# Six heads of a decay-attention kernel go from whole to split scores; where a split head's copies and subtractions run is changed

## The chip, the cores and the metric

One core of a Trainium2 chip runs the whole program. The metric is the device time of one execution in microseconds. Five engines are spoken of: PE (TensorE, matrix products), DVE (VectorE), ACT (ScalarE), POOL (GpSimd) and SP (SyncE, which issues the DMAs). Each engine works through its own instructions strictly in the order in which they stand; engines wait for each other through semaphores.

## The reference

For 8 batches of 8 heads, with 576 positions and 64 dimensions per head:

```
scores = q @ k.T / sqrt(64)
cum    = cumsum(log(clip(f, 1e-4, 1)))
attn   = softmax over s of: scores[t, s] + cum[t] - cum[s], with s <= t
x      = attn @ v                       (heads put side by side: 4608 tokens x 512)
out    = relu(x @ w_in)**2 @ w_out      (w_in 512 x 2048, w_out 2048 x 512)
```

All of it is float32, and the kernel keeps float32 accuracy.

## The kernel before, in words

**Whole and split.** PE multiplies float32 in two ways here. A *whole* product takes float32 operands as they are; the profile shows it as two MATMUL instructions for one product, and it is slow for each column. A *split* product writes an operand x as xh + xl, where xh is x rounded to the type float32r (a CAST) and xl = x - xh (a subtraction, itself written as float32r), and multiplies the parts, each in one fast pass. The weights, the MLP's activations and heads 16 to 63 are split; heads 0 to 15 are whole (`NWHOLE = 16`).

**Scores of a head.** `score` (line 383) makes the transposed scores of a head in six units, by blocks of keys, of 320, 320, 192, 64, 448 and 256 columns. A whole head takes one float32 product a unit (L392, keys and queries in tile `rl`). A split head takes two products a unit: kl0 by r2 (L399: rounded keys and rounded queries, tile `rk`, with rows for the cumulative decay and the row maximum), and l2 by r1 (L402: tile `rl`, 128 rows, where l2 holds the keys' low part above and the rounded keys below, and r1 the rounded queries above and the queries' low part below). So for a split head, `prep` (line 305) needs four copies, r2, kl0, the lower half of l2 and the upper half of r1, and two subtractions, the upper half of l2 and the lower half of r1. Before, DVE makes r2 and kl0 (L313, L314), ACT makes the two further copies (L315, L318), and POOL makes both subtractions (L321, L324).

**Maxima.** The row maximum of each head is taken ahead of its scores, while the head before it is scored. `max_units` (line 337) multiplies a block of r2 (as the stationary operand) by kl0 on PE (L346), and DVE reduces the result (L354); it does six such units for a head. For a split head the maxima go by DMA into a row of r2 (L359). For a whole head `turn_maxima` (line 371) turns them into a row with five small products on PE (L377) and two ACT copies (L381).

**Weights of the attention.** ACT takes the exponential (L409). Split heads mask the diagonal block on POOL afterwards (L411), cast p to its high part on ACT (L424), subtract on DVE (L425) and multiply by a split v (L435 to L437). Whole heads add the mask on PE ahead of the exponential (L395) and multiply whole p by whole v (L456). At the end of a half head ACT copies the result and the denominators out of PSUM (L470, L471). `split_v` (line 326) splits v with a cast on DVE (L332) and a subtraction on POOL (L333).

**MLP.** Tokens go in 18 chunks of 256, each with 16 steps of two halves: `mlp1` (twelve matmuls at L555, then ACT L563, DVE L564, ACT L565, DVE L566) and `mlp2` (six matmuls of 512 columns at L578).

**Conversion.** The weights come in a 64-bit form. `weight_ops` (line 186) turns each of 32 blocks into float32 words on DVE (L228, L233, L236, L240) with a magnitude on ACT (L205); then ACT casts the high part (L210) and POOL subtracts for the low part (L216). An MLP step is written only after its two blocks' low parts are.

**What sets the order.** The main loop (from line 742) goes by slots, one score unit each, six to a head. In slot n it writes: the score of this unit, the product with v of two slots earlier, divisions, events of the slot's first half, conversion, MLP halves as a pace demands (`fill`), events of the second half, conversion, MLP halves. Events are fixed by tables (lines 632 to 636): `SPLIT = 0, 1, 1, 3` puts the four parts of `prep` of head h into the second halves of slots 0, 1, 1 and 3 of head h - 1; `MAXIMA` puts the six maximum units of a split head at slots 1.5 to 4, and those of a whole head at 0 to 2.5. Within one half slot `prep` is written ahead of the maximum unit. `in_order` keeps PE, ACT, DVE and POOL in the order of writing. So the order on each engine is fixed, and a wait on one instruction holds all that follows on that engine.

Of the kernel before, what the change touches and what calls it, by code (L numbers as in the profile page):

```python
# [9 lines left out]
F32 = mybir.dt.float32  # L10
# [4 lines left out]
ALU = mybir.AluOpType  # L15
# [19 lines left out]
def decay_attention_relu2_kernel(  # L35
# [35 lines left out]

    MAG_LOW, MAG_HIGH = struct.unpack("<2f", struct.pack("<2I", 0x38000000, 0x47EFFFFF))

    NWHOLE = 16
    DEPTH = 4
    cpool = ctx.enter_context(tc.tile_pool(name="cpool", bufs=1))
    wk = ctx.enter_context(tc.tile_pool(name="wk", bufs=2))
# [54 lines left out]
    def f32(x):  # L132
        return x if x.dtype == F32 else x.bitcast(F32)
# [52 lines left out]
    def weight_ops():  # L186

        staged, done = {}, {}

        def stage():  # L190
            i = len(staged)
            if i < NW:
                raw = staged[i] = wk.tile([P, 2 * DM], I32, name=f"w{i}", bufs=1)
                nc.sync.dma_start(out=raw, in_=(w_in, w_out)[i % 2][i // 2].bitcast(I32))

        def words(i):
            w = staged[i].rearrange("p (n t) -> p n t", t=2)
            return w[:, :, 0], w[:, :, 1]

        mags = {}  # L200

        def magnitude(i):
            if i < NW:
                mags[i] = wk.tile([P, DM], F32, name="wmag", bufs=1)
                nc.scalar.activation(out=mags[i], in_=words(i)[1].bitcast(F32), func=AF.Abs)  # L205

        def high_part(i):
            if i >= 0:
                hl = wk.tile([P, 2, DM], F32R, name=f"w{i}", bufs=1)
                nc.scalar.copy(out=hl[:, 0], in_=done[i])  # L210
                done[i] = done[i], hl

        def low_part(i):
            if i >= 0:
                w, hl = done.pop(i)
                nc.gpsimd.tensor_tensor(out=hl[:, 1], in0=w, in1=hl[:, 0].bitcast(F32), op=ALU.subtract)  # L216
                split_w.append(hl)

        stage()
        yield  # L220
        magnitude(0)
        stage()
        yield
        for i in range(NW):
            low, high = words(i)
            mag = mags.pop(i)

            nc.vector.tensor_scalar(mag, mag, MAG_LOW, MAG_HIGH, ALU.max, ALU.min)  # L228
            yield
            w = done[i] = wk.tile([P, DM], F32, name="osb")  # L230
            wi = w.bitcast(I32)

            nc.vector.tensor_scalar(wi, mag.bitcast(I32), 3, 0x3FFFFFFF, ALU.logical_shift_left, ALU.bitwise_and)  # L233
            high_part(i - 1)
            yield
            nc.vector.scalar_tensor_tensor(wi, high, -0x40000000, wi, ALU.bitwise_and, ALU.bitwise_or)  # L236
            low_part(i - 1)
            magnitude(i + 1)
            yield
            nc.vector.scalar_tensor_tensor(wi, low, 29, wi, ALU.logical_shift_right, ALU.bitwise_or)  # L240
# [57 lines left out]
    def load_v(h):  # L298
        if h < NH:
            vr = state[h]["vr"] = wk.tile([P, NJ, D + 2], F32, name="v", bufs=3)  # L300
            nc.sync.dma_start(out=vr[:, :, :D], in_=v[h])
            if h < NWHOLE:
                nc.gpsimd.memset(vr[:, :, D:], 1.0)

    def prep(h, part):

        if part == 0:
            x = planes(wk, F32R, "rl")
            (r2, kl0), (r1, l2) = ((x.q, x.k) for x in (rounded[h % 2], x))
# [3 lines left out]
            nc.vector.tensor_copy(out=r2[:D], in_=st["raw"][:, 0, :])  # L313
            nc.vector.tensor_copy(out=kl0[:D, :S], in_=st["raw"][:, 1, :])  # L314
            nc.scalar.copy(out=st["l2"][D:, :S], in_=st["raw"][:, 1, :])  # L315
        st = state[h]
        if part == 1:
            nc.scalar.copy(out=st["r1"][:D], in_=st["raw"][:, 0, :])  # L318
        if part == 2:
            k, l2 = st["raw"][:, 1, :], st["l2"][:D, :S]  # L320
            nc.gpsimd.tensor_tensor(out=l2, in0=k, in1=st["kl0"][:D, :S].bitcast(F32), op=ALU.subtract)  # L321
        if part == 3:
            q, r1 = st["raw"][:, 0, :], st["r1"]
            nc.gpsimd.tensor_tensor(out=r1[D:], in0=q, in1=r1[:D].bitcast(F32), op=ALU.subtract)  # L324

    def split_v(h):
        if NWHOLE <= h < NH:
            st = state[h]
            vr = st["vr"][:, :, :D]
            vh = st["vh"] = vhs[h % 2]  # L330
            st["vl"] = wk.tile([P, NJ, D], F32R, name="v", bufs=3)
            nc.vector.tensor_copy(out=vh[:, :, :D], in_=vr)  # L332
            nc.gpsimd.tensor_tensor(  # L333
                out=st["vl"], in0=vr, in1=vh[:, :, :D].bitcast(F32), op=ALU.subtract,
            )
# [47 lines left out]
    def score(h, u):  # L383
        st = state[h]
        j, q0, q1 = UNITS[u]
        k0, kn = KT[j]
        n = q1 - q0
        ps = bank("s")
        if h < NWHOLE:
            masked = q0 == k0  # L390
            r, k = st["whole"].q[:D + 3], st["whole"].k[:D + 3]
            nc.tensor.matmul(ps[:kn, :n], k[:, k0:k0 + kn], r[:, q0:q1], start=True, stop=not masked)  # L392
            if masked:
                m = min(kn, n)
                nc.tensor.matmul(  # L395
                    ps[:kn, :m], mz[:kn, MW - P:MW - P + kn], eye[:kn, :m], start=False, stop=True,
                )
        else:
            nc.tensor.matmul(  # L399
                ps[:kn, :n], st["kl0"][:D + 3, k0:k0 + kn], st["r2"][:D + 3, q0:q1], start=True, stop=False,  # L400
            )
            nc.tensor.matmul(  # L402
                ps[:kn, :n], st["l2"][:, k0:k0 + kn], st["r1"][:, q0:q1], start=False, stop=True,
            )
        if h < NWHOLE:
            p = wk.tile([P, 448], F32, name=("ph", "pl")[u % 2], bufs=3)
        else:
            p = wk.tile([P, 448], F32, name="p")
        nc.scalar.activation(out=p[:kn, :n], in_=ps[:kn, :n], func=AF.Exp, scale=SCALE)  # L409
        if h >= NWHOLE and q0 == k0:  # L410
            nc.gpsimd.affine_select(  # L411
                out=p[:kn, :min(kn, n)], in_=p[:kn, :min(kn, n)], pattern=[[1, min(kn, n)]],
                compare_op=ALU.is_ge, fill=0.0, base=0, channel_multiplier=-1,
            )
        st["p"][u] = p
# [23 lines left out]
    def av_part(h, u, low):  # L439

        j, q0, q1 = UNITS[u]
        s0, s1 = (q0, min(q1, QA)) if low else (max(q0, QA), q1)
        if s0 >= s1:
            return
        st = state[h]
        first = u == (NU - 1 if low else 0)
        last = u == NU - 2
        if first:
            st["av"] = bank("av")
        acc = st["av"]  # L450
        kn = KT[j][1]
        base = 0 if low else QA
        o, i = slice(s0 - base, s1 - base), slice(s0 - q0, s1 - q0)
        if h < NWHOLE:
            vr = st["vr"][:kn, j, :D + 1]
            nc.tensor.matmul(acc[:D + 1, o], vr, st["p"][u][:kn, i], start=first, stop=last)  # L456
        else:
            av_split(st, acc, u, o, i, first, last)
        if last:
            n = QA if low else S - QA  # L460
            if not low:
                if h % H == 0:
                    xts[h // H] = wk.tile([P, NCC, S], F32, name=f"xt{h // H % 2}", bufs=1)
                if h % 2 == 0:
                    st["den"] = wk.tile([P, S], F32, name="den")
                else:
                    st["den"] = state[h - 1]["den"]
            o = (h % 2) * D
            x = xts[h // H][o:o + D, (h % H) // 2, base:base + n]
            nc.scalar.copy(out=x, in_=acc[:D, :n])  # L470
            nc.scalar.copy(out=st["den"][o:o + 1, base:base + n], in_=acc[D:D + 1, :n])  # L471
# [270 lines left out]
    for n in range(-2 * NU, last_slot + 1):  # L742
        live = 0 <= n < len(slots)
        split_last()
        if live:
            h, u = slots[n]
            score(h, u)
            if h >= NWHOLE:
                unsplit.append((h, u))
        for ha, ua in avs.get(n, ()):  # L750
            if ua < NU - 1:
# [59 lines left out]
```

## Time and profile before

| | us |
|---|---|
| runs: median (lowest to highest) of 3 | 1220.62 (1219.54 to 1220.74) |
| the profiled execution | 1217.56 |
| its span, first to last instruction | 1215.8 |
| PE busy | 1189.4 (98%) |
| weight loads on PE (beside the matmuls) | 1047.3 (86%) |
| DVE busy | 769.5 (63%) |
| ACT busy | 706.2 (58%) |
| POOL busy | 361.8 (30%) |

Busy time of PE counts matmuls whose ends are modelled and which overlap in the pipeline, so how fast PE advances is better read from the start of one matmul to the start of the next. A timeline row gives the start, the duration, the engine, the line, the operation, the tiles (out<-in) and the shape; in brackets stands the idle time of the engine ahead of it and what ended it. "x8" means that eight equal instructions are merged. A windows row gives the window, then busy time and count of PE, PEld, DVE, ACT and POOL, the granted PE clock (1.00 is full speed), DMA share and GB/s. A group row gives the count, busy time, mean duration in ns, and idle time ahead of the group.

### The profile page before, as it was taken

Reading aid. Unit: us, or ns where it says so; the run is one execution under the profiler, and the core shown is the slowest. Engines: PE = TensorE matmul, PEld = TensorE weight load, DVE = VectorE, ACT = ScalarE, POOL = GpSimd, SP = SyncE. Lnnn points to the kernel's source line nnn. Section 1 sums busy time; section 2 is a strip of 40 time slices with the busy share of each in tenths; the row PEclk is TensorE's granted clock in tenths of the full one; section 3 lists DMA queues with packets and bytes.
Section 4 is the critical chain, followed back from the end, with each engine's and each line's share of the span. In section 5 each row is a group of like instructions: output and inputs, shape, how many; then the busy total and the mean of one; then the engine's idle time right before and its main releaser. Section 6 shows DMA issues by size and latency. Waiting matters only on the chain.

```text
span 1215.8 us, 23255 instructions
## 1 busy us (share of the span) xinstructions
PE 1189.4 (98%) x7816; PEld 1047.3 (86%) x7816; DVE 769.5 (63%) x2031; ACT 706.2 (58%) x1736; POOL 361.8 (30%) x551
## 2 busy tenths in 40 slices
PE   6999999899999999999999999999999999999998
PEld 3668787779999898999999989988999899999997
DVE  5767776766767667665655766667676767533332
ACT  3875556566666666655556566666666666533232
POOL 3332322333334333322322333333333333200000
PEclk8999999999999999999999999999999999999999
DMA  7889310111211112111121212212121212000000
GB/s 217 206 198 272 90 42 26 47 46 42 59 42 53 38 47 50 41 49 27 43 55 21 53 32 44 57 42 58 37 50 33 58 43 58 12 28 11 9 18 18
DMA packets 104767, 72.16 MB, mean 59 GB/s; under 512 B 86573, under 2 KB 86573, under 8 KB 104649
## 3 DMA queue, kind: packets, MB, share of 16 engines
q1 hardware_dynamic: 103368, 65.96, 21.2%
q0 software_dynamic: 1280, 4.72, 1.6%
q8 instruction: 62, 1.02, 0.4%
q14 instruction: 57, 0.46, 0.1%
HBM read 60.51 MB, written 9.87 MB: 58 GB/s over the span
## 4 chain that ended last, share of the span: by engine, by line
PE 90%; ACT 4%; DVE 2%; issue 2%; DMA 1%; POOL 0%; SPq 0%; DVEq 0%; POOLq 0%; ACTq 0%
PE bank L555 33%; PE bank L578 31%; PE bank L346 4%; PE bank L392 3%; PE bank L435 3%; PE bank L456 3%; PE bank L402 3%; PE bank L437 3%; PE bank L436 3%; PE bank L399 3%; ACT r L563 1%; DVE bank L354 1%; ACT gh L565 0%; ACT den L471 0%; ACT p L409 0%
## 5 line engine op out<-in xcount | busy, mean ns | idle before, releaser
L578 PE MATMUL bank<-w,gh 128*128 128x512 f32 x1152 | 414.1, 400 | 0.0
L555 PE MATMUL bank<-xh,w 128*128 128x256 f32 x2304 | 329.0, 285 | 1.9 <-POOL w L216 1.9
L555 PEld LDWEIGHTS bank<-xh,w 128*128 128x128 f32 x2304 | 300.3, 189 | 10.3 <-POOL w L216 2.4
L425 DVE TENSOR_TENSOR pl<-p,ph 128x320 fp32r<-128x320 f32 (+4 forms) x288 | 177.4, 616 | 192.8 <-ACT ph L424 188.3
L578 PEld LDWEIGHTS bank<-w,gh 128*128 128x128 f32 x1152 | 217.5, 189 | 38.4
L563 ACT ACTIVATE r<-bank 128x256 f32<-128x256 f32 x288 | 110.6, 384 | 218.4 <-PE bank L555 172.3
L578 PE MATMUL bank<-w,gl 128*128 128x512 f32 x576 | 226.9, 394 | 0.2 <-DVE gl L566 0.2
L564 DVE TENSOR_TENSOR g<-r 128x256 f32<-128x256 f32 x288 | 125.7, 437 | 146.6 <-ACT r L563 146.0
L424 ACT CAST ph<-p 128x320 fp32r<-128x320 f32 (+4 forms) x288 | 119.4, 415 | 145.6 <-POOL p L411 103.0
L411 POOL TENSOR_SCALAR_AFFINE_SELECT p<-p 128x128 f32<-128x128 f32 (+1 forms) x240 | 77.1, 321 | 412.0 <-ACT p L409 317.6
L555 PE MATMUL bank<-xl,w 128*128 128x256 f32 x1152 | 184.5, 282 | 0.0
L555 PEld LDWEIGHTS bank<-xl,w 128*128 128x128 f32 x1152 | 158.2, 191 | 0.2 <-DVE xl L543 0.2
L566 DVE TENSOR_TENSOR gl<-g,gh 128x256 fp32r<-128x256 f32 x288 | 130.3, 452 | 36.2 <-ACT p L409 2.0
L354 DVE CUSTOM_DVE_ANT_0 bank<-bank,mz 128x256 f32<-128x256 f32 (+4 forms) x320 | 133.4, 433 | 22.6 <-PE bank L346 20.5
L409 ACT ACTIVATE p<-bank 128x320 f32<-128x320 f32 (+4 forms) x288 | 111.6, 388 | 60.1 <-PE bank L402 48.9
L565 ACT ACTIVATE gh<-r 128x256 fp32r<-128x256 f32 x288 | 120.6, 419 | 9.4
L346 PE MATMUL bank<-rk 66*128 66x320 f32 (+4 forms) x384 | 110.6, 317 | 13.9 <-DVE tcol L354 11.0
L578 PEld LDWEIGHTS bank<-w,gl 128*128 128x128 f32 x576 | 109.3, 190 | 14.4 <-DVE gl L566 0.9
L435 PE MATMUL bank<-pl,vh 128*65 128x320 f32 (+4 forms) x336 | 93.3, 278 | 2.6 <-ACT den L471 2.6
L346 PEld LDWEIGHTS bank<-rk 66*128 66x128 f32 (+1 forms) x384 | 67.2, 181 | 29.3 <-DVE tcol L354 13.0
L436 PE MATMUL bank<-ph,v 128*64 128x320 f32 (+4 forms) x336 | 91.2, 271 | 0.0
L437 PE MATMUL bank<-ph,vh 128*65 128x320 f32 (+4 forms) x336 | 89.3, 272 | 0.0
(92 smaller groups left out, 1539.0 us busy)
## 6 DMA issues: line engine op xcount, KB each, us to landing
qkraw<-in_qk SPq DMA_DIRECT2D x48, 288.0 KB
v<-in_v SPq DMA_DIRECT2D x64, 160.0 KB
out<-osb SPq DMA_DIRECT2D x36, 256.0 KB
den<-rdr SPq DMA_DIRECT2D x62, 144.0 KB
w<-in_w_in SPq DMA_DIRECT2D x16, 512.0 KB
w<-in_w_out SPq DMA_DIRECT2D x16, 512.0 KB
rl<-in_qk SPq DMA_DIRECT2D x16, 288.0 KB
rk<-in_qk POOLq DMA_DIRECT2D x16, 288.0 KB, 4.4
```

The source lines that it names most:

```text
L346: nc.tensor.matmul(ps[:m, :n], st["r2"][:D + 2, q0:q0 + m], st["kl0"][:D + 2, k0:k0 + n], start=True, stop=True,)
L354: nc.vector.tensor_tensor_reduce(out=ps[:m, :n], in0=ps[:m, :n], in1=mz[:m, mo:mo + n], op0=ALU.add, op1=ALU.min, scale=-1.0, scalar=init, ...
L425: nc.vector.tensor_tensor(out=pl[:kn, :n], in0=p[:kn, :n], in1=ph[:kn, :n].bitcast(F32), op=ALU.subtract,)
L435: nc.tensor.matmul(acc[:D + 1, o], vh, pl[:kn, i], start=first, stop=False)
L436: nc.tensor.matmul(acc[:D, o], vl, ph[:kn, i], start=False, stop=False)
L437: nc.tensor.matmul(acc[:D + 1, o], vh, ph[:kn, i], start=False, stop=last)
L555: nc.tensor.matmul(ph[:, :T], w[:, s, cc], x[:, cc, :], start=(cc == 0 and k == 0), stop=(cc == NCC - 1 and k == 2),)
L563: nc.scalar.activation(out=r, in_=ph[:, :T], func=AF.Relu)
L564: nc.vector.tensor_tensor(out=g, in0=r, in1=r, op=ALU.mult)
L565: nc.scalar.activation(out=gh, in_=r, func=AF.Square)
L566: nc.vector.tensor_tensor(out=gl, in0=g, in1=gh.bitcast(F32), op=ALU.subtract)
L578: nc.tensor.matmul(po, g[:, ts], w[:, s], start=(fc == 0 and k == 0), stop=(fc == NF - 1 and k == 2),)
```

## The change

It has four parts.

1. Heads 10 to 15 take split scores (`NWHOLE = 10`), but keep whole p and v and the mask on PE (`NPLAIN = 16`). They no longer load a whole copy of q and k or turn maxima on PE; their maxima move to the split heads' slots, and they go through `prep`.
2. In `prep`, for all split heads (now 10 to 63), ACT makes the rounded copies themselves: kl0 in part 0 and r2 in part 1. The second copies (the lower half of l2, the upper half of r1) are DMAs from kl0 and r2, issued on SP.
3. Both subtractions of `prep` go from POOL to DVE, in their old slots.
4. The conversion's subtraction goes from POOL to DVE and is written one step later.

```diff
-    NWHOLE = 16
+    NWHOLE = 10
+    NPLAIN = 16
...
-                nc.gpsimd.tensor_tensor(out=hl[:, 1], in0=w, in1=hl[:, 0].bitcast(F32), op=ALU.subtract)
+                nc.vector.tensor_tensor(out=hl[:, 1], in0=w, in1=hl[:, 0].bitcast(F32), op=ALU.subtract)
...
             nc.vector.scalar_tensor_tensor(wi, high, -0x40000000, wi, ALU.bitwise_and, ALU.bitwise_or)
-            low_part(i - 1)
             magnitude(i + 1)
             yield
             nc.vector.scalar_tensor_tensor(wi, low, 29, wi, ALU.logical_shift_right, ALU.bitwise_or)
+            low_part(i - 1)
...
             nc.gpsimd.memset(f32(x.k[:, S:]), 0.0)
-            nc.vector.tensor_copy(out=r2[:D], in_=st["raw"][:, 0, :])
-            nc.vector.tensor_copy(out=kl0[:D, :S], in_=st["raw"][:, 1, :])
-            nc.scalar.copy(out=st["l2"][D:, :S], in_=st["raw"][:, 1, :])
+            nc.scalar.copy(out=kl0[:D, :S], in_=st["raw"][:, 1, :])
+            nc.sync.dma_start(out=f32(l2[D:, :S]), in_=f32(kl0[:D, :S]))
         st = state[h]
+        q, k = (st["raw"][:, i, :] for i in range(2))
         if part == 1:
-            nc.scalar.copy(out=st["r1"][:D], in_=st["raw"][:, 0, :])
+            nc.scalar.copy(out=st["r2"][:D], in_=q)
+            nc.sync.dma_start(out=f32(st["r1"][:D]), in_=f32(st["r2"][:D]))
         if part == 2:
-            k, l2 = st["raw"][:, 1, :], st["l2"][:D, :S]
-            nc.gpsimd.tensor_tensor(out=l2, in0=k, in1=st["kl0"][:D, :S].bitcast(F32), op=ALU.subtract)
+            nc.vector.tensor_tensor(
+                out=st["l2"][:D, :S], in0=k, in1=st["kl0"][:D, :S].bitcast(F32), op=ALU.subtract,
+            )
         if part == 3:
-            q, r1 = st["raw"][:, 0, :], st["r1"]
-            nc.gpsimd.tensor_tensor(out=r1[D:], in0=q, in1=r1[:D].bitcast(F32), op=ALU.subtract)
+            nc.vector.tensor_tensor(out=st["r1"][D:], in0=q, in1=st["r2"][:D].bitcast(F32), op=ALU.subtract)
...
+        masked = q0 == k0
+        added = masked and h < NPLAIN
         if h < NWHOLE:
...
+            nc.tensor.matmul(ps[:kn, :n], k[:, k0:k0 + kn], r[:, q0:q1], start=True, stop=not added)
...
-                ps[:kn, :n], st["l2"][:, k0:k0 + kn], st["r1"][:, q0:q1], start=False, stop=True,
-            )
-        if h < NWHOLE:
+                ps[:kn, :n], st["l2"][:, k0:k0 + kn], st["r1"][:, q0:q1], start=False, stop=not added,
+            )
...
+        if added:
+            nc.tensor.matmul(
+                ps[:kn, :m], mz[:kn, MW - P:MW - P + kn], eye[:kn, :m], start=False, stop=True,
+            )
+        if h < NPLAIN:
             p = wk.tile([P, 448], F32, name=("ph", "pl")[u % 2], bufs=3)
```

Where `NWHOLE` decided on whole p and v, `NPLAIN` now stands. The lines of the changed kernel are two or three further down: L315 and L318 of before are now L314 and L319, L346 is L348, L399 and L402 are L397 and L400.

**ACT while head 43 is scored.** These are ACT's instructions as `prep` of head 44 passes; `rk` is the tile of r2 and kl0, `rl` that of r1 and l2, `p` and `ph` belong to head 43. What an instruction waits for stands in brackets. Before:

```order
L315 CAST rl_9679<-qkraw_9610 64x576 [waits DMAHW5_49]
L424 CAST ph_9685<-p_9670 128x320 [waits Activation_49]
L563 ACTIVATE r_9702<-bank4_9689 128x256 [waits DVE_49,PE_49]
L565 ACTIVATE gh_9704<-r_9702 128x256 [waits Activation_49]
L409 ACTIVATE p_9713<-bank1_9710 128x320 [waits PE_49]
L470 COPY xt1_9154<-bank0_9716 64x256 [waits PE_49]
L471 COPY den_9675<-bank0_9716 1x256
L424 CAST ph_9725<-p_9713 128x320 [waits Pool_49]
L318 CAST rl_9679<-qkraw_9610 64x576
L409 ACTIVATE p_9744<-bank3_9741 128x192 [waits DVE_49,PE_49]
```

And of the changed kernel:

```order
L314 CAST rk_0_79<-qkraw_9664 64x576 [waits DMAHW6_49,DMAHW2_49]
L427 CAST ph_9738<-p_9724 128x320 [waits Activation_49]
L566 ACTIVATE r_9755<-bank4_9742 128x256 [waits DVE_49,PE_49]
L568 ACTIVATE gh_9757<-r_9755 128x256 [waits Activation_49]
L412 ACTIVATE p_9766<-bank1_9763 128x320 [waits PE_49]
L473 COPY xt1_9208<-bank0_9769 64x256 [waits PE_49]
L474 COPY den_9729<-bank0_9769 1x256
L427 CAST ph_9778<-p_9766 128x320 [waits Pool_49]
L319 CAST rk_0_79<-qkraw_9664 64x576 [waits DMAHW0_49]
L412 ACTIVATE p_9798<-bank3_9795 128x192 [waits DVE_49,PE_49]
```

ACT's order is the same; its two casts at these places now write `rk` where they wrote `rl`.

**PE at the same place.** These are PE's instructions around the first maximum unit of head 44, the one of 128x256 from `rk`. Before:

```order
L578 MATMUL bank7_9374<-w13_1239,gh_9655 128x512
L346 MATMUL bank2_9738<-rk_0_79 128x256 [waits DMAHW3_49,DVE_49]
L399 MATMUL bank3_9741<-rk_1_80 128x192
L402 MATMUL bank3_9741<-rl_9434 128x192
L435 MATMUL bank0_9747<-pl_9686,vh_1_84 65x320 [waits DVE_49,PE_49,Activation_49]
```

And of the changed kernel:

```order
L581 MATMUL bank7_9428<-w13_1235,gh_9709 128x512
L348 MATMUL bank2_9792<-rk_0_79 128x256 [waits DMAHW7_49,Activation_49]
L397 MATMUL bank3_9795<-rk_1_80 128x192
L400 MATMUL bank3_9795<-rl_9488 128x192
L438 MATMUL bank0_9801<-pl_9739,vh_1_84 65x320 [waits DVE_49,PE_49]
```

PE's order is the same here; the first maximum unit waited for DVE (and a DMA), and now waits for ACT: the awaited instruction is the cast at L319 shown above.

**PE around head 11's first maximum unit.** Head 10 is scored here, with MLP halves of chunk 0 between. Before:

```order
L555 MATMUL bank_1346<-xh_1113,w_805 128x256 x8
L555 MATMUL bank_1346<-xl_1114,w_805 128x256 x4
L392 MATMUL bank_1372<-rl 128x320
L456 MATMUL bank_1232<-ph,v 65x320
L346 MATMUL bank_1380<-rk_80 128x256
```

And of the changed kernel:

```order
L558 MATMUL bank_1395<-xh_1110,w_970 128x256 x8
L558 MATMUL bank_1395<-xl_1111,w_970 128x256 x4
L397 MATMUL bank_1416<-rk_79 128x320
L400 MATMUL bank_1416<-rl 128x320
L405 LDWEIGHTS mz
L405 MATMUL bank_1416<-p,mz 128x128
L459 MATMUL bank_1422<-pl,v 65x256
L459 MATMUL bank_1422<-ph,v 65x128
L348 MATMUL bank_1437<-rk_80 128x256
```

The unit moved one slot later, and the score ahead of it is two products in place of one; the MLP halves stand in the order in which they stood.

More of the change, by code (lines that the diff above doesn't have):

```diff
@@ L312, in prep @@
             nc.gpsimd.memset(f32(x.k[:, S:]), 0.0)
-            nc.vector.tensor_copy(out=r2[:D], in_=st["raw"][:, 0, :])
-            nc.vector.tensor_copy(out=kl0[:D, :S], in_=st["raw"][:, 1, :])
-            nc.scalar.copy(out=st["l2"][D:, :S], in_=st["raw"][:, 1, :])
+            nc.scalar.copy(out=kl0[:D, :S], in_=st["raw"][:, 1, :])
+            nc.sync.dma_start(out=f32(l2[D:, :S]), in_=f32(kl0[:D, :S]))
         st = state[h]
+        q, k = (st["raw"][:, i, :] for i in range(2))
         if part == 1:
-            nc.scalar.copy(out=st["r1"][:D], in_=st["raw"][:, 0, :])
+            nc.scalar.copy(out=st["r2"][:D], in_=q)
+            nc.sync.dma_start(out=f32(st["r1"][:D]), in_=f32(st["r2"][:D]))
         if part == 2:
-            k, l2 = st["raw"][:, 1, :], st["l2"][:D, :S]
-            nc.gpsimd.tensor_tensor(out=l2, in0=k, in1=st["kl0"][:D, :S].bitcast(F32), op=ALU.subtract)
+            nc.vector.tensor_tensor(
+                out=st["l2"][:D, :S], in0=k, in1=st["kl0"][:D, :S].bitcast(F32), op=ALU.subtract,
+            )
         if part == 3:
-            q, r1 = st["raw"][:, 0, :], st["r1"]
-            nc.gpsimd.tensor_tensor(out=r1[D:], in0=q, in1=r1[:D].bitcast(F32), op=ALU.subtract)
+            nc.vector.tensor_tensor(out=st["r1"][D:], in0=q, in1=st["r2"][:D].bitcast(F32), op=ALU.subtract)
     def split_v(h):
-        if NWHOLE <= h < NH:
+        if NPLAIN <= h < NH:
             st = state[h]
@@ L388, in score @@
         ps = bank("s")
+        masked = q0 == k0
+        added = masked and h < NPLAIN
         if h < NWHOLE:
-            masked = q0 == k0
             r, k = st["whole"].q[:D + 3], st["whole"].k[:D + 3]
[L392 to L396, printed above, removed]
-                )
+            nc.tensor.matmul(ps[:kn, :n], k[:, k0:k0 + kn], r[:, q0:q1], start=True, stop=not added)
         else:
@@ L402, in score @@
             nc.tensor.matmul(
-                ps[:kn, :n], st["l2"][:, k0:k0 + kn], st["r1"][:, q0:q1], start=False, stop=True,
+                ps[:kn, :n], st["l2"][:, k0:k0 + kn], st["r1"][:, q0:q1], start=False, stop=not added,
             )
-        if h < NWHOLE:
+        m = min(kn, n)
+        if added:
+            nc.tensor.matmul(
+                ps[:kn, :m], mz[:kn, MW - P:MW - P + kn], eye[:kn, :m], start=False, stop=True,
+            )
+        if h < NPLAIN:
             p = wk.tile([P, 448], F32, name=("ph", "pl")[u % 2], bufs=3)
@@ L409, in score @@
         nc.scalar.activation(out=p[:kn, :n], in_=ps[:kn, :n], func=AF.Exp, scale=SCALE)
-        if h >= NWHOLE and q0 == k0:
+        if masked and not added:
             nc.gpsimd.affine_select(
-                out=p[:kn, :min(kn, n)], in_=p[:kn, :min(kn, n)], pattern=[[1, min(kn, n)]],
+                out=p[:kn, :m], in_=p[:kn, :m], pattern=[[1, m]],
                 compare_op=ALU.is_ge, fill=0.0, base=0, channel_multiplier=-1,
@@ L453, in av_part @@
         o, i = slice(s0 - base, s1 - base), slice(s0 - q0, s1 - q0)
-        if h < NWHOLE:
+        if h < NPLAIN:
             vr = st["vr"][:kn, j, :D + 1]
@@ L747, in decay_attention_relu2_kernel @@
             score(h, u)
-            if h >= NWHOLE:
+            if h >= NPLAIN:
                 unsplit.append((h, u))
```

## Prediction

> **What bounds the kernel now.** First the windows view, a stretch of 30 us in the steady state; then the line that sums up the chain of waits.
>
> ```profile
> 540.00:570.00 30.00, 30.00 (x206) 27.42 (x205) 19.03 (x51) 15.60 (x39) 8.49 (x14) 1.00 0.16 37
> ```
> ```profile
> by line: PE bank L555 32.7%; PE bank L578 31.3%; PE bank L346 4.0%; PE bank L392 3.4%; PE bank L435 3.3%; PE bank L456 3.1%; PE bank L402 2.9%; PE bank L437 2.8%; PE bank L436 2.8%; PE bank L399 2.7%; issue 2.0%; ACT r L563 0.7%; DVE bank L
> ```
>
> PE is busy for 30.00 of 30 us while DVE, ACT and POOL are busy for 19, 16 and 8. So whatever shortens or stops PE's stream moves the end by as much, and what shortens the other three moves nothing unless PE waits for it. Two questions decide: what PE no longer has to do, and what it has to wait for that it did not wait for.
>
> **PE's saved work (heads 10 to 15).** By the chain, L392 (whole scores of 16 heads) takes 3.4% of 1215.8, 41.3 us or 2.58 a head; L399 and L402 (split scores of 48 heads) take 5.6%, 68.1 us or 1.42 a head. Six heads save 6 x 1.16 = **7.0 us**. The mask and p times v stay. These heads also stop turning maxima, L377. The timeline of PE shows one turn, and the start of the last one's second part with its wait:
>
> ```profile
> 146.19 0.85 PE L377 MATMUL bank<-p 128*65 128x128 f32 x5
> 146.88 1.19 PE L555 MATMUL bank<-xh,w 128*128 128x256 f32 x8
> ```
> ```profile
> 201.22 0.24 PE L377 MATMUL bank<-p 128*65 128x64 f32 x1 [1.27 <-ACT ph L409]
> ```
>
> A turn holds PE for 146.88 - 146.19 = 0.69 us; six make 4.1, and the 1.27 us of waiting goes with them: **5.4 us**. Both terms are fast PE work by the same engine, so I take them as they are.
>
> **PE's new wait (heads 16 to 63).** The first maximum unit of a head multiplies r2. Before, DVE made r2 a slot earlier; now ACT makes it in part 1 of `prep`, which stands in the same half slot right ahead of that unit, at the place where ACT made its second copy of q (L318). So the trace of before shows when the new producer will be done: when L318 ends. ACT's timeline around it, while head 43 is scored:
>
> ```profile
> 716.95 0.41 ACT L424 CAST ph<-p 128x256 fp32r<-128x256 f32 x1 [1.76 <-POOL p L411]
> 717.27 0.38 ACT L563 ACTIVATE r<-bank 128x256 f32<-128x256 f32 x1
> ...
> 722.10 0.37 ACT L471 COPY den<-bank 1x256 f32<-1x256 f32 x1
> 722.37 0.45 ACT L424 CAST ph<-p 128x320 fp32r<-128x320 f32 x1
> 722.73 0.67 ACT L318 CAST rl<-qkraw 64x576 fp32r<-64x576 f32 x1
> 723.42 0.33 ACT L409 ACTIVATE p<-bank 128x192 f32<-128x192 f32 x1
> ```
>
> And PE's, at the same moment:
>
> ```profile
> 722.08 0.28 PE L346 MATMUL bank<-rk 66*128 66x256 f32 x1
> 722.20 0.25 PE L399 MATMUL bank<-rk 67*128 67x192 f32 x1
> 722.29 0.28 PE L402 MATMUL bank<-rl 128*128 128x192 f32 x1
> 722.51 0.36 PE L435 MATMUL bank<-pl,vh 128*65 128x320 f32 x1
> ```
>
> PE reaches the unit at 722.08; L318 ends at 723.40. From 716.95 on ACT has no idle time in brackets: it works through a burst, and no wait in the burst is one that this change shortens. PE would stand for 1.32 us, with the whole of its stream (scores of head 43, products with v, MLP) queued behind. The other pairs, from the timelines of ACT and of PE: the first, one from the stretch where `mlp1` stands right ahead of the unit, and the last.
>
> ```profile
> 212.45 0.66 ACT L318 CAST rl<-qkraw 64x576 fp32r<-64x576 f32 x1
> ```
> ```profile
> 211.46 0.28 PE L346 MATMUL bank<-rk 66*128 66x256 f32 x1
> ```
> ```profile
> 557.73 0.66 ACT L318 CAST rl<-qkraw 64x576 fp32r<-64x576 f32 x1
> ```
> ```profile
> 556.79 0.28 PE L346 MATMUL bank<-rk 66*128 66x256 f32 x1
> ```
> ```profile
> 1033.47 0.67 ACT L318 CAST rl<-qkraw 64x576 fp32r<-64x576 f32 x1
> ```
> ```profile
> 1032.41 0.28 PE L346 MATMUL bank<-rk 66*128 66x256 f32 x1
> ```
>
> End of L318 less start of the unit: 1.65, 1.60 and 1.73 us. Over all 48 pairs it lies between 0.88 and 2.16, with a mean of 1.51. That makes 48 x 1.51 = **72.5 us**. PE starts some 0.04 us after its release (L435 at 722.51 after L471's end at 722.47): 48 x 0.04 = **1.9 us**. Does ACT lag further and further? The page's group of its first MLP step says no:
>
> ```profile
> L563 ACT ACTIVATE r<-bank 128x256 f32<-128x256 f32 x288 | 110.6, 384 | 218.4 <-PE bank L555 172.3
> ```
>
> Outside the bursts ACT idles for PE, 172 us in all; so it starts each head level with PE, and each head pays once. Something comes back: L435 at 722.51 stood behind L471; from L402 it took 0.22 us where L399 to L402, equally wide, took 0.09. With PE 1.3 us later that wait is gone: 48 x 0.13 = **6.2 us** returned.
>
> **The same wait for heads 10 to 15.** Before has no `prep` there. A head before these shows what ACT does between a score and the cast's new place:
>
> ```profile
> 135.35 0.44 ACT L409 ACTIVATE pl<-bank 128x320 f32<-128x320 f32 x1 [1.36 <-PE bank L395]
> ...
> 136.38 0.36 ACT L471 COPY den<-bank 1x256 f32<-1x256 f32 x1
> 136.66 0.61 ACT L210 CAST w<-osb 128x512 fp32r<-128x512 f32 x1
> ```
> ```profile
> 135.72 0.45 PE L346 MATMUL bank<-rk 66*128 66x448 f32 x1
> ```
>
> Where no MLP half stands between (heads 11, 13, 15 in the order), PE would be at the unit at about 135.72, and ACT, with the cast of 0.67 behind 137.27, done at 137.94: 2.2 us. Where `mlp2` stands between (heads 10 and 14), PE comes its 1.4 us later: some 0.8. Head 12 has `mlp1` ahead, 1.6 as at 556.79. Sum 3 x 2.2 + 2 x 0.8 + 1.6 = **9.8 us**; ends 3 (0.5 each) and 15.
>
> **DVE's and POOL's work.** The groups:
>
> ```profile
> L216 POOL TENSOR_TENSOR w<-osb,w 128x512 fp32r<-128x512 f32 x32 | 43.5, 1360 | 90.3 <-ACT w L210 90.3
> L313 DVE CAST rk<-qkraw 64x576 fp32r<-64x576 f32 x48 | 27.6, 575 | 0.0
> L314 DVE CAST rk<-qkraw 64x576 fp32r<-64x576 f32 x48 | 30.1, 628 | 0.0
> L425 DVE TENSOR_TENSOR pl<-p,ph 128x448 fp32r<-128x448 f32 x48 | 29.9, 624 | 30.0 <-ACT ph L424 29.8
> L170 DVE TENSOR_TENSOR qkraw<-xt,qkraw 64x576 fp32r<-64x576 f32 x1 | 0.8, 751 | 0.0
> ```
>
> DVE loses 0.58 + 0.63 and gains two subtractions like L170's, 1.50: 0.3 us more a head, and DVE has 11 us free in 30. Its first maximum unit comes after the new subtraction, but PE arrives there 1.3 us later too. The conversion's subtraction costs DVE 512/448 of L425's 0.62, 0.71 us, 32 times, 23 us in the first 230. It can hold a maximum unit on which L377 waits, in heads 1 to 9 (0 to 0.5 us each): I take **1.5 us**, ends -1 (POOL no longer beside it) and 5.
>
> **The DMA copies** are issued when ACT's casts end. The one landing time on the page and the start of the score that needs them:
>
> ```profile
> rk<-in_qk POOLq DMA_DIRECT2D x16, 288.0 KB, 4.4
> ```
> ```profile
> 734.04 0.31 PE L402 MATMUL bank<-rl 128*128 128x320 f32 x1
> ```
>
> 723.4 + 4.4 = 727.8, six us ahead of 734.04; the load of maxima and of v on SP's queue behind them has as much. Nothing. Were that cover gone, each us of lateness would cost 54.
>
> **The clock.** A wait of PE can cost more than its length:
>
> ```profile
> 252.32 0.41 PE L346 MATMUL bank<-rk 66*128 66x320 f32 x1 [2.16 <-DVE tcol L354]
> ```
> ```profile
> 254.00:258.00 4.00, 4.00 (x18) 3.21 (x17) 1.45 (x4) 2.05 (x5) 0.00 (x0) 0.67 0.03 3
> ```
>
> After an idle time of 2.16 us the clock was granted at 0.67 in the next 4 us: about 1.3 us lost. After the 1.27 us at 201.22 nothing of the kind. Most new waits are near the short one; with three of 2.2 us in heads 11 to 15, I take **4 us**, ends 0 and 54 x 1.3 = 70. The Trainium skill ("TensorE: Matmul & The Clock Gate", What's actually happening) has the clock halved only after an idle window of some 3.4 us; by that, this term would be nothing. Here 2.16 us did it, so the measurement decides.
>
> **The sum.** 1217.6 - 7.0 - 5.4 + 72.5 + 1.9 - 6.2 + 9.8 + 1.5 + 4 = 1288.7 for a profiled execution. Before's stands 3.1 us below its median (1220.62 less 1217.56), so the forecast is **1292 us**, 5.8% slower.
>
> **The rivals.**
>
> *Faster: ACT is released earlier.* ACT's burst begins when POOL lets go of it (1.76 us at 716.95). If POOL, freed of two subtractions a head, let the burst begin 1.5 us sooner, the cast would land ahead of PE, and only the savings stay: 1217.6 - 7.0 - 5.4 + 1.5 = 1206.7, a median of 1210. It decides once the burst begins 1.5 us earlier. For it: the waits on POOL. Against it, DVE's and POOL's timelines one head on:
>
> ```profile
> 731.51 0.35 DVE L332 CAST vh<-v 128x320 fp32r<-128x320 f32 x1
> ```
> ```profile
> 732.00 0.88 POOL L333 TENSOR_TENSOR v<-v,vh 128x320 fp32r<-128x320 f32 x1 [1.66 <-PE bank L435]
> 732.83 0.29 POOL L411 TENSOR_SCALAR_AFFINE_SELECT p<-p 128x128 f32<-128x128 f32 x1
> ```
>
> POOL idles 1.66 us, then subtracts v behind L332, then masks: none of it is touched. Chance 0.05.
>
> *Half of it is absorbed.* If the freed DVE lets ACT and PE drift so that waits halve to 0.75 us: 1292 - 36 = 1256. Nothing in the rows does this; 0.08.
>
> *The clock falls at most waits:* 1292 + 66 = 1358 if at all 54, 1325 if at half. One row speaks for it, the 1.27 us against. 0.08.
>
> *The change does not do what it says:* if PE waited for r2 only later than the first unit, nothing would be paid; the order shows that unit waiting for ACT. 0.01, together with a result near 1220.
>
> **How the numbers follow.** The forecast has 0.78. Its own ends: 1292 with stalls at the low bound for heads 10 to 15, no clock term and twice the time returned, 1292 - 7 - 4 - 6 = 1275; and with the high bounds and the clock falling at a dozen waits, 1292 + 5 + 4 + 16 = 1317. The range reaches down into the half-absorbed case, to 1262. Outside stay the faster one, most of the clock's and the lower part of the half-absorbed. A measurement of this kernel tells about 0.2% from no change: faster 0.05, same 0.02, slower 0.93 (the 0.02 are the rival without effect and the last of the half-absorbed one).
>
> **What would show it.** In the changed profile PE L348 (66x256) idles 54 times, about 1.3 us each (the idle time counts from the end of the matmul before), released by ACT at L319; PE's tenths fall to 9 or 8; L377 counts 50 in place of 80; L402's successor no longer waits for L474. Wrong if L319 ends before PE comes to that unit, if PE's busy share stays at 98%, or if the clock is granted below 0.97.

## The result, and the profile after

The changed kernel takes 1290.28 us (median of four runs, 1283.65 to 1293.96) where the kernel before takes 1220.68 (four runs): a ratio of 1.0573, 95% interval [1.0547, 1.0599]. It is 5.7% slower. The profiled execution took 1293.96 us, with a span of 1292.1 and a mean granted clock of 0.983 (before: 0.994). One execution of run 2 below took 2318.5 us, for no reason that its record shows, and is left out of that run's figures.

First the engines' busy time from the profile page, and PE's busy tenths in 40 slices of the span:

```profile
PE 1199.3 (93%) x7786; PEld 1049.1 (81%) x7786; DVE 761.7 (59%) x2075; ACT 703.7 (54%) x1736; POOL 175.0 (14%) x423
PE   7999988989999999999899999999999999999998
```

PE's share fell from 98% to 93%; no slice has a hole, a few show 8, and the rest of the loss hides within the nines (90% or more). POOL's busy time halved (361.8 before), and nothing came of that: the end is set by PE. So the question is what PE stood for. The view of waits, PE's rows, says it in one line (engine, tile and line that waited, what released it; total us, times, longest); behind it the two rows of the kernel before that are compared with it:

```profile
PE bank L348 <- ACT rk L319: 71.0, 54, 2.3
PE bank L348 <- DVE tcol L356: 10.4, 4, 6.8
```
```profile
PE bank L346 <- DVE tcol L354: 11.0, 4, 7.2
PE bank L435 <- ACT den L471: 2.6, 8, 0.4
```

There are 54 waits, one for each split head, each for ACT's cast of q into r2 (L319): 71.0 / 54 = 1.31 us of idle time. The wait of the same line for DVE was there before (11.0, then L346) and stays. The groups of the page, for the step itself, for ACT's first MLP step and for the product with v that follows the second score product:

```profile
L348 PE MATMUL bank<-rk 66*128 66x320 f32 (+4 forms) x384 | 116.5, 332 | 84.2 <-ACT rk L319 71.0
L566 ACT ACTIVATE r<-bank 128x256 f32<-128x256 f32 x288 | 110.5, 384 | 253.0 <-PE bank L558 228.0
L438 PE MATMUL bank<-pl,vh 128*65 128x320 f32 (+4 forms) x336 | 91.4, 272 | 0.0
```

ACT itself now idles longer for PE than before (228.0 us in place of 172.3). It is not short of time; it is late at one place in each head, and PE, late from then on, makes ACT wait elsewhere. The 2.6 us for which the v product stood before (then L435) are gone, as PE comes later.

The moment at which head 43 is scored again, PE first (start, duration, instruction, in brackets the idle time ahead and what ended it), then ACT; the last row is PE's last MLP matmul ahead of the unit in the kernel before:

```profile
774.24 0.39 PE L581 MATMUL bank<-w,gh 128*128 128x512 f32 x1
775.59 0.39 PE L348 MATMUL bank<-rk 66*128 66x256 f32 x1 [0.97 <-ACT rk L319]
775.82 0.25 PE L397 MATMUL bank<-rk 67*128 67x192 f32 x1
```
```profile
774.24 0.36 ACT L474 COPY den<-bank 1x256 f32<-1x256 f32 x1
774.51 0.45 ACT L427 CAST ph<-p 128x320 fp32r<-128x320 f32 x1
774.87 0.67 ACT L319 CAST rk<-qkraw 64x576 fp32r<-64x576 f32 x1
776.22 0.33 ACT L412 ACTIVATE p<-bank 128x192 f32<-128x192 f32 x1 [0.68 <-PE bank L400]
```
```profile
721.84 0.40 PE L578 MATMUL bank<-w,gh 128*128 128x512 f32 x1
```

The cast ends at 775.54 and PE starts at 775.59. Start to start the MLP's last matmul and the maximum unit stand 1.35 us apart; before it was 722.08 - 721.84 = 0.24. So this head pays 1.11 us, of which the bracket shows 0.97. The order on ACT is the one forecast: copies out of PSUM, cast of p, cast of q, with no idle time between them.

What PE's waits do to the clock is seen in the windows view (window, busy time of PE, PEld, DVE, ACT and POOL with counts, granted clock, DMA share, GB/s), in two pairs of neighbouring stretches of 3.4 us:

```profile
423.10:426.50 3.40, 1.66 (x13) 1.50 (x13) 2.11 (x6) 2.27 (x7) 0.62 (x2) 1.00 0.23 51
426.50:429.90 3.40, 3.40 (x15) 3.07 (x14) 1.58 (x6) 0.99 (x3) 0.00 (x0) 0.50 0.09 14
1037.50:1040.90 3.40, 1.79 (x14) 1.77 (x15) 2.12 (x7) 2.21 (x6) 0.43 (x2) 1.00 0.21 45
1040.90:1044.30 3.40, 3.40 (x24) 3.06 (x24) 2.23 (x9) 1.27 (x4) 0.24 (x1) 1.00 0.04 5
```

PE was busy for 1.66 us of the first stretch and got half the clock in the next; with 1.79 us it kept the whole clock, and did 24 matmuls where it did 15. The record of the granted clock has 13 such half-rate stretches of 3.41 us in this execution, and 4 in the one of before. Seven of the 13, and one of the 4, stand behind a stretch in which PE idled for 1.6 us or more; the others are at the start and at some 90 us.

### The profile page after: what moved, and what is told of

It is laid out like the page before. It is cut to its first block, busy times and chain, and to the rows that moved or that the text cites. A ratio compares the mean times of both kernels' runs of the same rounds, so it can differ in the third digit from the quotient of the medians.

```text
span 1292.1 us, 23500 instructions
## 1 busy us (share of the span) xinstructions
PE 1199.3 (93%) x7786; PEld 1049.1 (81%) x7786; DVE 761.7 (59%) x2075; ACT 703.7 (54%) x1736; POOL 175.0 (14%) x423
## 5 line engine op out<-in xcount | busy, mean ns | idle before, releaser
L558 PEld LDWEIGHTS bank<-xh,w 128*128 128x128 f32 x2304 | 303.6, 191 | 9.7 <-ACT w L211 2.1
L428 DVE TENSOR_TENSOR pl<-p,ph 128x320 fp32r<-128x320 f32 (+4 forms) x288 | 128.4, 446 | 221.1 <-ACT ph L427 202.3
L566 ACT ACTIVATE r<-bank 128x256 f32<-128x256 f32 x288 | 110.5, 384 | 253.0 <-PE bank L558 228.0
L348 PE MATMUL bank<-rk 66*128 66x320 f32 (+4 forms) x384 | 116.5, 332 | 84.2 <-ACT rk L319 71.0
L427 ACT CAST ph<-p 128x320 fp32r<-128x320 f32 (+4 forms) x288 | 119.1, 413 | 137.2 <-POOL p L414 96.8
L348 PEld LDWEIGHTS bank<-rk 66*128 66x128 f32 (+1 forms) x384 | 67.7, 183 | 118.1 <-ACT rk L319 91.2
L414 POOL TENSOR_SCALAR_AFFINE_SELECT p<-p 128x128 f32<-128x128 f32 (+1 forms) x240 | 74.3, 309 | 627.4 <-ACT p L412 580.1
L569 DVE TENSOR_TENSOR gl<-g,gh 128x256 fp32r<-128x256 f32 x288 | 135.8, 472 | 35.4 <-PE bank L581 0.5
L400 PE MATMUL bank<-rl 128*128 128x320 f32 x324 | 95.5, 295 | 0.0
L397 PE MATMUL bank<-rk 67*128 67x320 f32 x324 | 93.7, 289 | 0.0
```

What stands on the lines that cost most here:

```text
L348: nc.tensor.matmul(ps[:m, :n], st["r2"][:D + 2, q0:q0 + m], st["kl0"][:D + 2, k0:k0 + n], start=True, stop=True,)
L400: nc.tensor.matmul(ps[:kn, :n], st["l2"][:, k0:k0 + kn], st["r1"][:, q0:q1], start=False, stop=not added,)
L427: nc.scalar.copy(out=ph[:kn, :n], in_=p[:kn, :n])
L428: nc.vector.tensor_tensor(out=pl[:kn, :n], in0=p[:kn, :n], in1=ph[:kn, :n].bitcast(F32), op=ALU.subtract,)
L558: nc.tensor.matmul(ph[:, :T], w[:, s, cc], x[:, cc, :], start=(cc == 0 and k == 0), stop=(cc == NCC - 1 and k == 2),)
L566: nc.scalar.activation(out=r, in_=ph[:, :T], func=AF.Relu)
```

## The experiments

The theory: the 48 waits, and six more in heads 10 to 15, for the r2 that ACT casts right ahead of PE's use, are the whole loss. Rival A: ACT's and DVE's added work is the loss. Rival B: the DMA copies or the split of heads 10 to 15 are. Rival C: ACT's burst is too long wherever the cast stands in it.

**1. r2 on DVE again.** One cast goes back to DVE and to part 0, as before; all the rest of the change stays.

```diff
+            nc.vector.tensor_copy(out=r2[:D], in_=st["raw"][:, 0, :])
             nc.scalar.copy(out=kl0[:D, :S], in_=st["raw"][:, 1, :])
...
         if part == 1:
-            nc.scalar.copy(out=st["r2"][:D], in_=q)
             nc.sync.dma_start(out=f32(st["r1"][:D]), in_=f32(st["r2"][:D]))
```

> The changed kernel, with the cast of r2 alone given back to DVE, in part 0 of prep; kl0 stays on ACT, both second copies stay DMAs, all subtractions stay on DVE, heads 10 to 15 stay split. Theory (PE waits at the first maximum unit for ACT's cast of r2, 71 us of idle time in 54 waits, and the clock drops that come of it, some 12 us): the idle time there goes below 5 us, the granted clock goes from 0.983 back to 0.993 or more, and the time is about 1208 us (1200 to 1214), below the kernel before, since the savings of heads 10 to 15 (some 12 us) stay. Rival A (the DMA copies or DVE's new subtractions cost the time, and the wait only shows it): at least 1250. Rival B (another wait takes its place, on kl0, which ACT makes too): 1225 to 1260, with a new releaser ahead of L348 or L397.

1211.77 us (1209.95 to 1216.96), ratio 0.9938 [0.9917, 0.996]. The place of one instruction in each head is worth 78 us, and with that instruction back in its old place the change is slightly faster than the kernel before, by 0.6%. PE's waits now:

```profile
PE bank L348 <- DVE tcol L356: 16.9, 8, 6.9
PE bank L438 <- ACT den L474: 2.2, 7, 0.4
```

No row names a cast of r2 any more; DVE carries 54 casts more and PE does not wait for those. B falls, and so does A for DVE; for ACT, which has 54 casts less here, run 3 decides. The 5.9 us more of waiting for DVE (11.0 before) come up again in runs 5 and 8.

**2. The cast twice.** ACT casts q into r1 too, right ahead of the cast into r2.

```diff
         if part == 1:
+            nc.scalar.copy(out=st["r1"][:D], in_=q)
             nc.scalar.copy(out=st["r2"][:D], in_=q)
-            nc.sync.dma_start(out=f32(st["r1"][:D]), in_=f32(st["r2"][:D]))
```

> The changed kernel, but ACT also makes r1 by a cast of q of its own (0.67 us in the trace of before), right ahead of the cast into r2, in place of the DMA copy of r2. Theory (PE stands at the first maximum unit of 54 heads until ACT has made r2, so anything put ahead of that cast is paid once a head): 54 x 0.67 = 36 us more, 1290 + 36 = 1326, and up to 1365 if the longer waits (about 2 us each) also drop the clock. Rival (the cost of the change lies in DVE's and ACT's added work or in the DMA copies, not in this wait): 1285 to 1300, since ACT is busy for only 54% of the span.

1350.17 us (the median of three, and the profiled execution), ratio 1.1068 [1.1034, 1.1103]: 60 us more than the change. The same wait, and one pair of stretches:

```profile
PE bank L348 <- ACT rk L320: 102.3, 54, 2.9
```
```profile
1085.50:1088.90 3.40, 1.08 (x8) 0.70 (x6) 1.87 (x4) 2.66 (x7) 0.32 (x1) 1.00 0.17 36
1088.90:1092.30 3.40, 3.40 (x18) 3.36 (x15) 1.03 (x5) 0.73 (x3) 0.29 (x1) 0.51 0.04 5
```

The wait grew by 31.3 us, 0.58 a head for a cast of 0.67. The rest is the clock: 0.961 on the mean, 29 half-rate stretches from 60 us on, where the changed kernel has 10. Span times mean clock, an estimate of the time at full clock, takes the clock out: 1348.5 x 0.961 = 1295.9 against 1292.1 x 0.983 = 1270.1, a difference of 25.8, which leaves some 31 of the 56.4 us between the two spans to the clock. The dose rules out that the wait is a mere label; and a wait that gets longer by half costs nearly twice as much.

**3. The maximum unit half a slot later**, with ACT's cast where the change put it.

```diff
-    MAXIMA = (0, 0.5, 1, 1.5, 2, 2.5), (1.5, 2, 2.5, 3, 3.5, 4)
+    MAXIMA = (0, 0.5, 1, 1.5, 2, 2.5), (2, 2, 2.5, 3, 3.5, 4)
```

> The changed kernel, with the first maximum unit of a split head half a slot later (2 in place of 1.5), the other five where they were; no work moves between engines. Theory: PE comes to that unit 0.9 us later where an mlp2 half or nothing stands ahead of it, and 1.4 us or more later where an MLP half comes between, so of the waits some 0.4 to 0.5 us are left in some 40 heads, and none in 8: about 20 us of idle time in place of 71, and 1228 us (1215 to 1242). Rival A (the moved work costs the time): 1285 to 1295. Rival B (the maxima then come too late on DVE for the banks or the scores): above 1242 with DVE as the releaser.

1236.84 us, ratio 1.0137 [1.0103, 1.0171]. Most of the loss goes, though ACT does all of the work that it does in the changed kernel; so A falls for ACT too. Not all of it goes:

```profile
PE bank L348 <- ACT rk L319: 15.7, 42, 0.7
```

With 0.37 us a wait, the clock of the profiled execution stays at 0.996 and no stretch after 92 us is at half rate. The run is 25.1 us above run 1, and the idle time in the row is only 15.7, since part of the wait lies under the modelled end of the matmul ahead. Start to start, the 54 units stand 31.1 us in all behind the matmul ahead of them; the other units stand 0.12 us behind the same matmul (L440) and 0.18 behind L459, which would make 7 us for these 54. So the shorter wait itself accounts for most of the 25 us.

**4. ACT's cast half a slot earlier**, in part 1 at slot 0 in place of slot 1.

```diff
-    SPLIT = 0, 1, 1, 3
+    SPLIT = 0, 0, 1, 3
```

> The changed kernel, with part 1 of prep (ACT's cast of r2 and the DMA behind it) in slot 0 in place of slot 1, nothing else. ACT does the same work, only earlier in its burst: the cast would end about 2.5 us earlier, PE comes to the unit 1.3 to 1.7 us ahead of where it ended. Theory: the wait goes in nearly all heads, idle time there below 8 us, time about 1209 us (1201 to 1216). Rival A (moved work): at least 1250. Rival C (ACT's burst as such is the limit: what stands behind the cast, the exponential of the next unit or the copies out of PSUM, now holds PE): 1220 to 1260, with ACT p, xt or den as releaser of PE.

1238.79 us, ratio 1.0143 [1.0112, 1.0174]. A miss: the wait for r2 is gone, but 1209 was expected. PE stands for ACT somewhere else:

```profile
PE bank L348 <- DVE tcol L356: 18.9, 9, 7.5
PE bank L438 <- ACT den L474: 17.7, 38, 0.9
```

In slot 0 both casts, of kl0 and of r2, stand ahead of ACT's copies of the result and the denominators out of PSUM, and PE's next product with v waits for the bank (2.6 us before). So C holds too, for ACT: at both places tried, 0.67 us added to the burst make something that PE needs come later. Run 1 shows that DVE has room for the cast.

**5. Part 1 alone**, on the kernel before: heads 10 to 15 with split scores, casts and subtractions as before.

```diff
-    NWHOLE = 16
+    NWHOLE = 10
+    NPLAIN = 16
```

> The kernel before, with part 1 of the change alone: heads 10 to 15 with split scores, whole p and v; prep's copies on DVE and ACT, its subtractions and the conversion's on POOL, as before. Theory (the savings are PE's: 7.0 us of faster scores and 5.4 us of maxima no longer turned): 1208 us (1203 to 1213). Rival (POOL, which then does two subtractions of 1.45 us a head beside the conversion's 1.36, or DVE with the conversion's steps beside two casts, holds PE in heads 10 to 15): 1214 to 1224, with POOL or DVE as releaser of PE between 90 and 250 us.

1227.19 us, ratio 1.0061 [1.0042, 1.0081]: slower by 0.6%, where the theory had 1208 and even the rival no more than 1224. PE's saved work is real: its busy time, counted at the granted clock, is 1175.8 us where it was 1184.0. But PE waits for DVE instead, in the stretch of these heads. The waits, and DVE's two-input step of the MLP between 90 and 270 us (count, busy, mean ns):

```profile
PE bank L347 <- DVE tcol L355: 22.2, 10, 7.2
```
```profile
L566 DVE TENSOR_TENSOR g<-r 128x256 f32<-128x256 f32 x33 | 22.0, 667 | 16.8 <-ACT r L565 16.8
```

The same step takes 471 ns in the kernel before and 425 in run 1. POOL is busy for 67 us of these 180 here, 54 before and 16 in run 1: the six heads put twelve more subtractions on POOL, beside the conversion's. Of the 33 steps, the 22 that no subtraction of POOL overlaps take 422 ns on the mean, and the 11 that one overlaps 1157.

**6. and 7. One kind of subtraction back on POOL**, in the kernel of run 1: the conversion's (6), or the two of `prep` (7).

```diff
-                nc.vector.tensor_tensor(out=hl[:, 1], in0=w, in1=hl[:, 0].bitcast(F32), op=ALU.subtract)
+                nc.gpsimd.tensor_tensor(out=hl[:, 1], in0=w, in1=hl[:, 0].bitcast(F32), op=ALU.subtract)
```

> The changed kernel with r2 back on DVE (1211.8), and the conversion's subtraction on POOL again, as before the change. Theory (a subtraction on POOL slows DVE's two-input operations beside it, and PE waits for DVE between 90 and 270 us): POOL busy some 55 us in that stretch in place of 16, DVE's two-input operations there longer, 1215 to 1220. Rival (DVE is short of time there, so 23 us less work for it helps): 1205 to 1210.

```diff
-            nc.vector.tensor_tensor(
+            nc.gpsimd.tensor_tensor(
                 out=st["l2"][:D, :S], in0=k, in1=st["kl0"][:D, :S].bitcast(F32), op=ALU.subtract,
...
-            nc.vector.tensor_tensor(out=st["r1"][D:], in0=q, in1=st["r2"][:D].bitcast(F32), op=ALU.subtract)
+            nc.gpsimd.tensor_tensor(out=st["r1"][D:], in0=q, in1=st["r2"][:D].bitcast(F32), op=ALU.subtract)
```

> The changed kernel with r2 back on DVE (1211.8), and the two subtractions of q and k of each split head on POOL again, as before the change. Theory (what made the split of heads 10 to 15 lose when it was made alone, 1227.2, is POOL's subtractions beside DVE's, in the stretch from 90 to 270 us): 1216 to 1222, PE's waits for DVE at the maximum units back to some 20 us. Rival (what made it lose was the conversion's subtraction on POOL alone): 1210 to 1213.

Run 6: 1222.72 us, ratio 1.0024 [1.0006, 1.0042]. Run 7: 1223.44, ratio 1.0025 [1.0006, 1.0044]. Each takes back some 11 us, though each relieves DVE, and both lie a little above the range of the theory. DVE's groups between 90 and 270 us, in run 1 and then in run 6; then one of run 7:

```profile
L217 DVE TENSOR_TENSOR w<-osb,w 128x512 fp32r<-128x512 f32 x21 | 14.3, 682 | 0.1
L234 DVE TENSOR_SCALAR osb<-wmag 128x512 int32<-128x512 int32 x20 | 9.6, 480 | 0.2
L229 DVE TENSOR_SCALAR wmag<-wmag 128x512 f32<-128x512 f32 x19 | 7.9, 418 | 0.0
```
```profile
L234 DVE TENSOR_SCALAR osb<-wmag 128x512 int32<-128x512 int32 x20 | 13.7, 684 | 3.8 <-POOL rl L313 3.3
L229 DVE TENSOR_SCALAR wmag<-wmag 128x512 f32<-128x512 f32 x19 | 13.3, 702 | 0.0
```
```profile
L567 DVE TENSOR_TENSOR g<-r 128x256 f32<-128x256 f32 x33 | 21.8, 659 | 21.2 <-ACT r L566 20.8
```

In run 6 the subtraction is off DVE (14.3 us less), but two other groups there take 9.5 us more; in run 7 it is the MLP's step, 659 ns in place of 425. A few long ones make this mean. One of them in run 7, POOL and then DVE, where DVE's next step of the same size is beside no subtraction:

```profile
200.10 1.48 POOL L326 TENSOR_TENSOR rl<-qkraw,rk 64x576 fp32r<-64x576 f32 x1
200.23 1.63 DVE L567 TENSOR_TENSOR g<-r 128x256 f32<-128x256 f32 x1
201.99 0.42 DVE L569 TENSOR_TENSOR gl<-g,gh 128x256 fp32r<-128x256 f32 x1
```

In run 7, the 7 of the 33 steps that overlap a subtraction of POOL take 1541 ns on the mean and the other 26 take 422; the mean of run 1 is 425. In run 6 the same holds of the conversion's step L229: 1191 ns (7) against 417 (12). The maximum of 448 columns, which DVE takes out of PSUM, is not slowed in run 6: 624 ns beside a subtraction (3), 627 otherwise (6).

The stretch as a whole, in run 1, run 6, run 7 and, last, the kernel before:

```profile
90.00:270.00 180.00, 166.56 (x1047) 139.37 (x1047) 139.34 (x352) 101.46 (x243) 15.57 (x35) 0.97 0.34 93
```
```profile
90.00:270.00 180.00, 161.91 (x975) 133.67 (x974) 135.17 (x313) 94.19 (x225) 39.30 (x50) 0.94 0.34 92
```
```profile
90.00:270.00 180.00, 160.83 (x973) 133.19 (x973) 137.56 (x318) 92.76 (x221) 42.52 (x47) 0.94 0.34 91
```
```profile
90.00:270.00 180.00, 170.85 (x1058) 140.45 (x1057) 129.40 (x305) 102.35 (x247) 54.09 (x60) 0.98 0.32 89
```

PE gets through 1047 matmuls with POOL at 16 us and through 975 and 973 with POOL at 39 and 43, and the clock falls from 0.97 to 0.94. PE's waits for DVE's maxima grow from 16.9 us to 20.6 and 21.2. POOL's load by itself is not the price: before, with heads 10 to 15 whole, PE gets through 1058 matmuls beside 54 us of POOL, while DVE, without the work of `prep` for these heads, is busy for 129 us in place of 139. So the price of a subtraction on POOL here is what it does to DVE where PE is next to wait for DVE. The Trainium skill ("SBUF — State Buffer", Who interferes with whom) says that DVE and GpSimd share a pair of ports, which DVE uses for a second input and in its fast copy and scalar modes; both kinds of rows, TENSOR_TENSOR and TENSOR_SCALAR, agree. That it is the ports and nothing else was not tried.

**8. Heads 10 to 15 whole**, in the kernel of run 1.

```diff
-    NWHOLE = 10
+    NWHOLE = 16
```

> The changed kernel with r2 back on DVE (1211.8), but heads 10 to 15 with whole scores, as before the change. It prices the split of these heads in the new arrangement of the other engines. By the prediction's two terms for them (7.0 + 5.4 saved, less nothing): 1224. By the start times of the heads in the run with r2 on DVE (4 to 5 us gained by head 16, the rest given back in waits of PE for DVE): 1216 to 1218. Rival (the split brings nothing; the gain came from the conversion's subtraction): 1211 to 1213.

1216.73 us, ratio 0.9972 [0.9951, 0.9992]. The split of these heads brings 5 us in the new arrangement, less than half of what the prediction gave it. The intervals of this run and of run 1 overlap a little (0.9951 to 0.996), but span times clock keeps the two apart: 1198.0 to 1201.0 in the ten executions of run 1, 1203.2 to 1208.3 in the twelve of this run. Its PE waits, to be held against run 1's:

```profile
PE bank L348 <- DVE tcol L356: 11.9, 4, 7.2
PE bank L438 <- ACT den L474: 2.1, 7, 0.4
```

With split heads PE waits for DVE 5.0 us longer (16.9), in eight places in place of four. Against the kernel before, this run prices the remaining edits, the cast of kl0 on ACT, the DMA copies and DVE's subtractions, together: a gain of 3 to 4 us (interval 1 to 6), where no r2 is late.

## Why the prediction came out right

The time (1292 forecast, 1290.28 measured) and its reason were right: run 1 takes one cast back and the whole loss goes with it. But several terms of the sum were off and made up for each other, so that a forecast within 2 us is in part luck. By its own steps:

| step | predicted | measured |
|---|---|---|
| wait for r2, heads 16 to 63, with the restart | +74.4 | +68.6, start to start, in the profiled execution |
| the v product's wait returned | -6.2 | -7.9 net, from the unit's start to the seventh matmul behind it; in it, the unit itself takes 4.6 more |
| the same wait, heads 10 to 15 | +9.8 | +10.4, start to start |
| split scores and turns saved | -12.4 | -5.0 (run 1 against run 8) |
| conversion's subtraction on DVE | +1.5 | no new wait; with the other edits -3 to -4 (run 8) |
| the clock | +4 | +9 in the medians, +15 in the profiled execution |

The measured terms make 68.6 - 7.9 + 10.4 - 5.0 - 3.5 + 9 = 71.6 us; the medians differ by 69.6. The three terms of the wait and the clock make 80.1 by themselves, and run 1, which takes the wait away, is 78.5 below.

**The wait** was read from the right pair of rows. Each head pays 1.43 us in place of 1.55. ACT's burst stands a little earlier against PE once PE is late: at head 43 the cast of p starts 0.27 us after the MLP's last matmul, where it started 0.53 after it. This is all that the half-absorbed rival got. For the six heads the idle times were 0.41, 2.29, 1.54, 1.52, 1.17 and 2.24 us (heads 10 to 15): heads 11 and 15, with no MLP half ahead, at 2.2 as forecast, head 13 lower.

**The savings** are the step that failed in size: 12.4 us forecast, 5.0 arrived. Taken "as they are", being work of the same engine, they ignored that a unit of PE's work that gets shorter lets PE reach the next wait sooner. In heads 10 to 15 DVE is the engine that is next. By the pages of run 1 and run 8, PE is busy for 5.0 us less with split heads (1178.8 against 1183.8) and idle for 3.3 more (31.3 against 28.0). Run 1's profile has two half-rate stretches there (at 229 and 250 us) that run 8's has not, and they hold some 3.4 us of the busy time; so the work itself is some 8 us less. Start to start and at full clock, the scores bring the 7.0 forecast, as the chain rows had it; the turns bring 3.3 where 5.4 was forecast, and the whole products with v behind them (L459) take 1.8 more, for a reason that is open. What is left of the 8 us is what the waits don't take back. The clock is no part of it over all executions: span times clock differs by 4.9 us between the medians of the two runs, as the times do.

**The clock** was undersized. The row behind the term was an idle time of 2.16 us with a lower clock behind it, and another of 1.27 without; where between them the limit lies was not known. It lies between 1.5 and 1.9 us of a 3.41 us stretch, and the new waits come up to it: in seven places of the changed kernel, 1.6 to 2.3 us of idle time within a stretch were followed by a half-rate stretch. The clock counted for 9 us, within the ends 0 and 70.

**What would show it** in the changed profile: 54 idle times released by L319, seen; PE's tenths at 9 and 8, seen; the v product's wait gone, seen; clock not below 0.97, 0.983. Turned maxima are 50 in place of 80 (L379 now). No wait of PE was ended by one of the DMA copies, as forecast. The rival in which ACT is released earlier fell: ACT's cast of p waits for POOL's mask 170 times for 96.8 us, where it was 171 times for 103.0, so a POOL with half its work gives ACT's burst no earlier start.

## What to carry to other kernels

On engines that work in order, the place of a producer counts, not the load of its engine: a cast of 0.67 us on an engine that idles for half the span cost 54 times 1.3 us because it was queued behind a burst right ahead of its use. Read from the trace of before when the instruction now standing at the new producer's place ends, and subtract the time at which the consumer starts. And credit saved work on the bounding engine only as far as no other engine is next in line at that place: here less than half of 12.4 us arrived.

## What the runs showed of the hardware

**The clock goes by stretches of 3.41 us.** From 110 us on, in the changed kernel and in run 2, every stretch in which PE idled for more than 1.9 of 3.41 us was followed by one at half rate, and none with less than 1.5 was, apart from one that directly followed another; between the two either came. The other traces agree. So the limit stands near half a stretch, and the same wait may or may not cross it, by how it falls on the grid. The Trainium skill ("TensorE: Matmul & The Clock Gate", What's actually happening) has the window of 3413 ns and half rate after an idle one; its window agrees with the trace, while here a window that was half idle was enough. The half-rate stretches at some 90 us, one to three of them in every trace but that of run 5, follow no idle time of PE: the first begins 64.85 us after the half-rate stretches at the start end, in each of the nine. They are not explained.

**Most of the spread of the runs is the clock.** The changed kernel's runs with spans of 1281.8 and 1292.1 had clocks of 0.989 and 0.983: span times clock is 1267.7 and 1270.1. In run 1, spans of 1208.2 to 1215.0 give 1198.0 to 1201.0. It does not hold everywhere: one execution of run 6 shows a clock of 0.941 at a span of 1219.8, in the middle of the others, whose clocks are 0.986 to 0.992. For the kernel before, 1215.8 x 0.994 = 1208.5. So of the 69.6 us between the medians some 60 are PE's own waiting and work, and 9 are clock.
